# Linear attention with a gated unit: a list schedule that knows one engine per PSUM bank and two DMA queues, K maxima and exponentials split by bank, gate taps built on GpSimd

## The chip, the cores and the metric

The kernel runs on one core of one Trainium2 chip. The metric is the device time of one execution in microseconds (us). Lower is better. Before the change the median of three runs was 279.94 us (273.2 to 291.83).

The engines are named as the profile names them. PE is the matrix engine, and PEld is its weight load. DVE is the vector engine, ACT the scalar engine, and POOL is GpSimd. SP only issues transfers here. PSUM is the memory that PE writes into. The kernel divides it into eight banks, and a piece of work takes one or two of them.

A run is called slow when it is more than 1.5% above the fastest of its kernel.

## The reference

Eight batches, eight heads, 576 rows, head size 64. Both q and k are mapped to 256 positive features, and linear attention follows. Its result goes through a gated unit with a causal convolution of five taps.

```python
def phi(x):
    proj = np.einsum('bhsd,df->bhsf', x, w_phi)
    proj = proj - np.max(np.abs(proj), axis=-1, keepdims=True)
    return np.concatenate([np.exp(proj), np.exp(-proj)], axis=-1)
q_p, k_p = (phi(q), phi(k))
kv  = np.einsum('bhsf,bhsd->bhfd', k_p, v);  z = np.sum(k_p, axis=2)
num = np.einsum('bhsf,bhfd->bhsd', q_p, kv)
den = np.einsum('bhsf,bhf->bhs', q_p, z)[..., None] + 1e-06
x = num / den                  # transposed to (batch, row, 512)
for k in range(5):
    gate_pre += conv_w[k][None, None, :] * xp[:, k:k + S, :]
out = (1 / (1 + np.exp(-gate_pre)) * (x @ w_val)) @ w_out
```

## The kernel before

The kernel is a program with a planner in it. Each piece of work is entered with its engine, an assumed cost, a priority and the buffers that it touches. A list scheduler then simulates the engines and fixes the order of every engine's instructions. Nothing of that is left at run time: each engine runs its own fixed list, in order.

A priority is made of the batch number times a period, plus a number per stage (`TURN`). The planner before assumed one transfer at a time, and it did not know that the program keeps two engines from being in one PSUM bank together:

```python
TURN = dict(
    kload=-55.6, qload=-18.1, vload=-18.1, wload=6.4, k=-4.5, q=1.3, kexp=-1.7, vs=-21.0, mqt=1.7, qp=10.0,
    kv=17.7, num=5.3, xt=16.6, gate=21.4, val=27.7, out=25.8,
)
# ... in Plan.run():
                    if o.dma:
                        dma_free = max(dma_free, now + cost + self.DMA_LAT - 1.0) + o.dma
                        end = dma_free + 1.0
```

The features of k come in five groups per batch, four whole ones and a tail of half the size. PE writes a group into two banks. DVE takes its absolute maximum, and ACT takes exp(+) and exp(-) of it. Each of the three instructions reads both banks:

```python
        def k_max(u, ps):
            # ...
            nc.vector.tensor_reduce(
                mem(MK[grp[u]])[:, 1, o:o + 2 * nx].rearrange("p (x t) -> p t x", t=2),
                mem(ps)[:, :, 0:nx * F].rearrange("p t (x f) -> p t x f", f=F),
                AX.X, ALU.max, apply_absolute_value=True)
        def k_exp(u, ps, sgn):
            # ...
            nc.scalar.activation(
                mem(KE[u])[:, sgn, :, :].rearrange("p (x t) f -> p t x f", t=2),
                mem(ps)[:, :, 0:nx * F].rearrange("p t (x f) -> p t x f", f=F), AF.Exp, scale=1.0 - 2.0 * sgn)
```

POOL scales v with exp of the negated maxima (`VT`), PE multiplies (`kv`), and so on to the output product. POOL also issues the loads that cast to bf16. For batches after the first, a load writes rows of k or q to a scratch (`KR`, `QR`), and SP issues a transposing transfer from there (`KT<-KR`). The first batch is transposed on PE, and DVE copies the result (`KT<-PS`). The taps of the gate (`GW`) are four multiplies made once, on DVE.

## Time and profile before

The profiled run took 274.97 us (a fast one), with a span of 273.1. These are lines of its page: busy time and share per engine; busy tenths in 40 equal slices; the granted clock in tenths; the busy share of the DMA engines; and the engines of the chain that ended last.

```profile
span 273.1 us, 8666 instructions
...
PE 216.7 (79%) x3756; PEld 165.4 (61%) x3756; DVE 176.5 (65%) x273; ACT 178.1 (65%) x234; POOL 113.6 (42%) x184
...
PE   0256758599988997979878997979798989898881
...
PEclk9999999979979998999989997999999999999998
DMA  7999999923999389818999779937960130022005
...
PE 40%; DVE 34%; ACT 10%; issue 7%; POOL 3%; DMA 1%; ACTq 1%; DVEq 0%
```

No engine is full, and the chain wanders between PE, DVE and ACT. The waits between them decide. The output product of the eight batches starts at 65.5, 94.8, 124.5, 154.5, 184.1, 212.7, 239.8 and 263.0 us. So the span is 65.5 us of start, seven steps (29.3, 29.7, 30.0, 29.6, 28.6, 27.1, 23.2), and 10.1 us at the end.

Here is a part of one batch, from the timeline of DVE before. The columns are start, length, engine, line, operation, output and inputs; the brackets give the idle time just before and what ended it.

```profile
175.42 1.22 DVE L476 TENSOR_REDUCE MK_83<-PS 128x8 f32<-128x1024 f32 x1
...
177.45 1.22 DVE L552 TENSOR_REDUCE MQ_100<-PS 128x8 bf16<-128x1024 f32 x1
180.22 0.69 DVE L476 TENSOR_REDUCE MK_83<-PS 128x4 f32<-128x512 f32 x1 [1.55 <-ACT KEt_80 L484]
```

And the timeline of ACT before in the same stretch:

```profile
176.73 1.94 ACT L484 ACTIVATE KE_74<-PS 128x1024 bf16<-128x1024 f32 x2 [1.25 <-DVE MK_83 L476]
178.55 0.66 ACT L747 ACTIVATE GS_127<-PS 128x576 bf16<-128x576 f32 x1
179.08 1.11 ACT L484 ACTIVATE KEt_80<-PS 128x512 bf16<-128x512 f32 x2
```

DVE and ACT take turns on the same group. ACT stands 1.25 us until the maximum of 175.42 has ended, and DVE stands 1.55 us until the exponentials of the tail have ended. The waits of PE between 70 and 245 us hold the same thing as a sum (total us, times, longest):

```profile
PE PS L446 <- ACT KE_74 L484: 6.1, 5, 1.4
PE PS L684 <- issue: 3.3, 3, 1.5
```

PE cannot write the next group until ACT has left the banks. "issue" is a stall that no instruction explains.

The start, on DVE: the taps come first, and the first maximum of k is at 17.37 us.

```profile
8.32 3.57 DVE L324 TENSOR_TENSOR GW<-ID_190,CO 128x768 bf16<-128x768 f32 x4
11.80 1.28 DVE L393 COPY KT_65<-PS 128x1024 bf16<-128x1024 bf16 x1
...
17.37 2.35 DVE L476 TENSOR_REDUCE MK_81<-PS 128x8 f32<-128x1024 f32 x2 [1.73 <-ACT KE_73 L484]
```

### The profile page before, as it was taken

The numbers are of one execution on the slowest core, as the hardware profiler recorded it, in microseconds if no ns is written. First come the engines' busy times: TensorE is split into PE (matmuls) and PEld (weight loads), VectorE is DVE, ScalarE is ACT, GpSimd is POOL, SyncE is SP. The second block draws the span as 40 slices with busy tenths as digits, with TensorE's granted clock in tenths as the row PEclk, the third lists the DMA queues.
The fourth block names the chain that finished last, engine by engine and source line by source line (L and its number), as shares of the span: only waits on it lengthen the run. The fifth ranks groups of instructions, "written<-read, shape, count | busy, mean of one in ns | idle before, by whom it ended". The sixth has DMA issues, their size and how long they took to land.

```text
span 273.1 us, 8666 instructions
## 1 busy us (share of the span) xinstructions
PE 216.7 (79%) x3756; PEld 165.4 (61%) x3756; DVE 176.5 (65%) x273; ACT 178.1 (65%) x234; POOL 113.6 (42%) x184
## 2 busy tenths in 40 slices
PE   0256758599988997979878997979798989898881
PEld 0244457466676766765756677666676577657750
DVE  2869407786479918875677837972897479726340
ACT  2048750498777797569947795689757995785311
POOL 8952790069134462419034735145142606260000
PEclk9999999979979998999989997999999999999998
DMA  7999999923999389818999779937960130022005
GB/s 95 139 274 246 167 157 265 157 51 93 226 206 191 72 208 270 195 25 192 204 200 179 160 188 246 120 89 186 239 100 0 72 105 2 4 87 92 2 0 173
DMA packets 59456, 38.80 MB, mean 142 GB/s; under 512 B 37402, under 2 KB 51098, under 8 KB 59354
## 3 DMA queue, kind: packets, MB, share of 16 engines
q1 hardware_dynamic: 47328, 25.37, 40.9%
q0 software_dynamic: 12000, 12.86, 28.6%
q8 instruction: 29, 0.48, 0.7%
q14 instruction: 9, 0.07, 0.1%
q10 hardware_dynamic: 90, 0.02, 0.0%
HBM read 30.49 MB, written 17.69 MB: 176 GB/s over the span
## 4 chain that ended last, share of the span: by engine, by line
PE 40%; DVE 34%; ACT 10%; issue 7%; POOL 3%; DMA 1%; ACTq 1%; DVEq 0%
PE PS L783 11%; PE PS L640 6%; PE PS L741 5%; PE PS L684 4%; DVE MK_82 L476 4%; PE PS L446 3%; PE PS L752 3%; ACT KE_74 L484 3%; DVE MK_81 L476 3%; DVE XN_117 L695 2%; DVE MQ_98 L552 2%; DVE MK_83 L476 2%; DVE MQ_100 L552 2%; DVE MQ_99 L552 2%; DVE XP_122 L724 2%
## 5 line engine op out<-in xcount | busy, mean ns | idle before, releaser
L484 ACT ACTIVATE KE_73<-PS 128x1024 bf16<-128x1024 f32 x16 | 15.7, 1028 | 30.4 <-PE PS L446 22.5
L752 PEld LDWEIGHTS <-WVAL 64*128 64x128 bf16 x512 | 26.9, 94 | 4.0 <-issue 0.6
L741 PEld LDWEIGHTS <-GW 128*64 128x64 bf16 x384 | 23.0, 115 | 7.2 <-issue 4.7
L476 DVE TENSOR_REDUCE MK_81<-PS 128x8 f32<-128x1024 f32 (+1 forms) x15 | 16.6, 1110 | 5.3 <-ACT KE_73 L484 2.0
L484 ACT ACTIVATE KE_74<-PS 128x1024 bf16<-128x1024 f32 x16 | 15.5, 1024 | 5.9 <-DVE MK_82 L476 2.6
L660 DVE CAST KVS_112<-PS 128x520 bf16<-128x520 f32 x8 | 5.2, 695 | 20.7 <-PE PS L652 17.3
L476 DVE TENSOR_REDUCE MK_82<-PS 128x8 f32<-128x1024 f32 (+1 forms) x13 | 14.2, 1096 | 6.0 <-PE PS L446 2.4
L752 PE MATMUL PS<-XP_122,WVAL 64*128 64x288 bf16 x256 | 17.9, 282 | 0.2 <-DVE MQ_100 L552 0.2
L503 POOL TENSOR_SCALAR MK_83<-MK_83 128x16 f32<-128x16 f32 (+1 forms) x5 | 1.3, 252 | 40.3 <-DVE MK_83 L476 28.7
L752 PE MATMUL PS<-XP_123,WVAL 64*128 64x288 bf16 x256 | 17.7, 282 | 0.0
L747 ACT ACTIVATE GS_124<-PS 128x576 bf16<-128x576 f32 x8 | 5.2, 655 | 18.9 <-PE PS L741 17.9
L741 PE MATMUL PS<-XP_123,GW 128*64 128x288 bf16 x192 | 15.2, 308 | 1.7 <-DVE XP_123 L724 1.0
L741 PE MATMUL PS<-XP_122,GW 128*64 128x288 bf16 x192 | 15.0, 297 | 1.5 <-DVE XP_122 L724 1.0
L476 DVE TENSOR_REDUCE MK_83<-PS 128x8 f32<-128x1024 f32 (+1 forms) x12 | 13.5, 1130 | 3.2 <-ACT KEt_80 L484 1.6
L503 POOL TENSOR_SCALAR MK_82<-MK_82 128x20 f32<-128x20 f32 (+1 forms) x5 | 1.3, 252 | 32.6 <-DVE MK_82 L476 32.6
L589 PEld LDWEIGHTS <-EB 64*128 64x128 bf16 x256 | 11.2, 100 | 4.2 <-issue 1.0
L609 ACT ACTIVATE QE_104<-PS 128x1024 bf16<-128x1024 f32 x12 | 11.8, 1032 | 1.7 <-PE PS L589 1.7
L552 DVE TENSOR_REDUCE MQ_100<-PS 128x8 bf16<-128x1024 f32 (+1 forms) x12 | 12.5, 1042 | 0.6 <-ACT GS_127 L747 0.3
L552 DVE TENSOR_REDUCE MQ_99<-PS 128x8 bf16<-128x1024 f32 (+1 forms) x12 | 12.4, 1041 | 0.5 <-PE PS L446 0.5
L609 ACT ACTIVATE QE_105<-PS 128x1024 bf16<-128x1024 f32 x12 | 11.7, 1030 | 1.5 <-PE PS L589 1.5
L446 PE MATMUL PS<-W_173,QT_67 64*128 64x128 bf16 x144 | 9.1, 242 | 4.4 <-issue 1.6
L660 DVE CAST KVS_113<-PS 128x520 bf16<-128x520 f32 x8 | 5.3, 695 | 10.6 <-PE PS L652 10.6
(284 smaller groups left out, 712.5 us busy)
## 6 DMA issues: line engine op xcount, KB each, us to landing
KR_141<-in_k_dram POOLq DMA_DIRECT2D x7, 512.0 KB, 8.0
QR_143<-in_q_dram POOLq DMA_DIRECT2D x7, 512.0 KB, 9.8
VN_69<-in_v_dram SPq DMA_DIRECT2D x6, 512.0 KB
VN_70<-in_v_dram SPq DMA_DIRECT2D x6, 512.0 KB, 4.1
out_dram<-OS_136 SPq DMA_DIRECT2D x9, 256.0 KB, 7.9
out_dram<-OS_138 SPq DMA_DIRECT2D x8, 256.0 KB, 4.2
out_dram<-OS_137 SPq DMA_DIRECT2D x7, 256.0 KB, 7.1
VN_69<-in_v_dram POOLq DMA_DIRECT2D x2, 512.0 KB, 8.3
```

What stands on the lines that cost most here:

```text
L446: nc.tensor.matmul(ps[:, par, F * x:F * x + F], Tt[ROWS[par], cols], W2[ROWS[par], :], start=True, stop=True,)
L476: nc.vector.tensor_reduce(mem(MK[grp[u]])[:, 1, o:o + 2 * nx].rearrange("p (x t) -> p t x", t=2), mem(ps)[:, :, 0:nx * F].rearrange("p t ( ...
L484: nc.scalar.activation(mem(KE[u])[:, sgn, :, :].rearrange("p (x t) f -> p t x f", t=2), mem(ps)[:, :, 0:nx * F].rearrange("p t (x f) -> p ...
L552: nc.vector.tensor_reduce(mem(MQ[j])[:, :].rearrange("p (t s) -> p t s", t=2)[:, :, o:o + n], mem(ps)[:, :, 0:n * F].rearrange("p t (x f) ...
L589: nc.tensor.matmul(mem(ps)[:, par, P * x:P * x + P], EB[ROWS[par], 4 * g + x, :], mem(MQS[j])[ROWS[par], :], start=False, stop=(x == 3), s ...
L609: nc.scalar.activation(mem(QE[u])[:, sgn, :, :, :], mem(ps).rearrange("p t (x i) -> p t x i", x=4), AF.Exp, scale=1.0 - 2.0 * sgn,)
L640: nc.tensor.matmul(mem(ps)[:, xi, c0:c0 + E1], mem(KE[u])[:, sgn, s, :], mem(VT[u])[:, sgn, s, :], start=(g == 0 and sgn == 0 and jp == 0) ...
L660: nc.vector.tensor_copy(mem(KVS)[:, 2 * xp:2 * xp + 2, :, :, :].rearrange("p x g s e -> p x (g s e)"), mem(ps)[:, :, 0:4 * E1],)
L684: nc.tensor.matmul(mem(ps)[0:m, g, x * E1:(x + 1) * E1], lhsT, mem(KVS)[:, x, g, sgn, :], start=(sgn == 0), stop=(sgn == 1),)
L741: nc.tensor.matmul(mem(ps)[ROWS[x], po, 0:HALF], GW[:, 2 * jt + x, po, s, :], mem(XP)[:, 2 * jt + x, s:s + HALF], start=(s == 0), stop=(s ...
L752: nc.tensor.matmul(mem(ps)[:, par, 0:HALF], WVAL[ROWS[par], h, jt * P:(jt + 1) * P], mem(XP)[ROWS[par], h, PAD:PAD + HALF], start=(h == 0) ...
L783: nc.tensor.matmul(mem(ps)[:, n, :], rows(jt)[:, P * c:P * c + P], WOUT[:, jt, :], start=(jt == 0), stop=(jt == 3),)
```

## The change

The intent is a better order, made possible by better knowledge in the planner. In its model a piece of work may not start while another engine is in its bank, and two DMA queues share the DMA engines, each of two transfers at half speed. K maxima and exponentials are halved, one bank each, so that DVE and ACT work on one group at the same time. The taps move from DVE to POOL. The copies of the first batch's K become contiguous, and the K groups read other columns to match. The priorities and some assumed costs were tuned anew. The core of the diff, with cuts:

```diff
+    def _transfers(self, until):
+        while True:
+            heads = [q for q in self.queues.values() if q and q[0][1] <= self.dma_now + 1e-9]
+            # ... each head moves at 1/len(heads) of full speed
+    def _can(self, o):
+        for t, k in o.banks:
+            for e, end in t.touch[k].items():
+                if e != o.eng and end > self.now:
+                    return False
+        return all(self._place(t) is not None for t in o.takes)
@@ priorities
-    kload=-55.6, qload=-18.1, vload=-18.1, wload=6.4, k=-4.5, q=1.3, kexp=-1.7, vs=-21.0, mqt=1.7, qp=10.0,
-    kv=17.7, num=5.3, xt=16.6, gate=21.4, val=27.7, out=25.8,
+    taps=2.5, kload=-50.4, qload=-16.3, vload=-11.0, wload=6.4, k=-4.5, q=1.3, kexp=-2.9, vs=-21.0, mqt=4.6,
+    qp=10.0, kv=17.3, num=5.3, xt=17.3, gate=21.4, val=27.5, out=35.3,
@@ taps
-            plan.op("DVE", 0.9, _At((0, "k", 10.0)), lambda jt=jt: build_gw(jt), w=[gw], after=[o])
+            plan.op("POOL", 1.55, _At((0, "taps", 3.0)), lambda jt=jt: build_gw(jt), w=[gw], after=[o])
@@ copies of the first K
-                mem(tok)[:, 8 * P * hh:8 * P * hh + 8 * P].rearrange("q (x i j) -> q x j i", x=4, j=2),
+                o.rearrange("q (x i j) -> q x j i", x=4, j=2) if i else o.rearrange("q (x j i) -> q x j i", x=4, j=2),
@@ K groups
-            plan.op("DVE", 1.13 * c, at("kexp") + p0, lambda u=u, ps=ps: k_max(u, ps), r=[ps], w=[MK[grp[u]]],
-                    takes=[MK[grp[u]]] if u in (0, 2) else [])
-            for sgn in range(2):
-                plan.op("ACT", 0.94 * c, at("kexp") + p0, lambda u=u, ps=ps, s=sgn: k_exp(u, ps, s), r=[ps], w=[KE[u]])
+            for par in range(2):
+                plan.op("DVE", 0.6 if u < 4 else 0.34, at("kexp") + p0, lambda u=u, ps=ps, p=par: k_max(u, ps, p),
+                        r=[ps], w=[MK[grp[u]]], takes=[MK[grp[u]]] if u in (0, 2) and par == 0 else [], bank=par)
+            for par in (1, 0):
+                for sgn in range(2):
+                    plan.op("ACT", 0.477 if u < 4 else 0.26, at("kexp") + p0,
+                            lambda u=u, ps=ps, s=sgn, p=par: k_exp(u, ps, s, p), r=[ps], w=[KE[u]], bank=par)
```

## The prediction

> **What bounds it now.** No engine is full: the page's first part has PE busy 79%, DVE 65%, ACT 65% of 273.1 us. The chain that ended last runs through PE 40%, DVE 34%, ACT 10%, issue 7%: waits between in-order queues. Key-value products start every 29.3, 29.6, 28.6 and 27.1 us (stretches 130 to 244.6 us); a stretch holds about 25 us of PE records, 20.6 of DVE, 22 of ACT.
>
> In the chain of one batch (159 to 189 us) PE is absent from 167.8 to 184.1 us: XN, XP, MQ_98, MK_83, MQ_98, MK_83 on DVE, two KE_74 exponentials (1.94 us) on ACT, the tail's exponentials (1.0), its maximum (0.69), then GV and the output product. DVE and ACT take turns on a K group: a maximum of 1.22 us and two exponentials of 1.94, 3.2 us in series, because they share PSUM banks. The Trainium skill ("PSUM — Partial Sum Buffer", PSUM bank collisions) says that two engines on one bank and quadrant collide even when both read; the trace agrees in that the waits view has MK waiting for KE and KE for MK, over 15 us in all. The old schedule planned them side by side.
>
> **What the change does.**
> 1. K group by bank: ACT takes bank 1 while DVE takes bank 0, then they swap; 3.2 us in series becomes about 2.1. Cost: a pair of 128x512 exponentials takes 1.11 us against 1.94, so halves add about 0.15 us a group, 0.6 to 0.7 us of ACT per batch; a 128x512 maximum is 0.69 against 1.22, so 0.4 to 0.7 us of DVE per batch. It should remove most of the 3.6 us in which DVE stands behind KE_74 and KEt. I count 2.3 us per batch, 16 us over seven.
> 2. Start: four GW multiplies (3.57 us on DVE, 8.3 to 11.9) hold up the first KT copy, whose transposes were done near 8.6. They go to POOL, an estimated 1.55 us each from its 1.04 for 128x512. The KT copies become contiguous (1.28 us to about 0.68, as the XP copy of that size). POOL scales the first two V groups before the second maximum, not after; VT now runs 29.0 to 38.6. I count 5 us.
> 3. The rest: PE's steady sequence is nearly the old one. I count 0. Matmuls and bytes are unchanged. The drain (28.5 us) gains nothing.
>
> **Sum.** 273 - 16 - 5 = 252 us for a fast run. Two of three runs before were 2.5% and 7% above their fastest, so I add some: **256 us**, 8 in 10 within **246 to 268**. Faster by over 2%: 0.91; within 2%: 0.07; slower: 0.02.
>
> **What would show it.** Step 1: the period falls from 29 to about 26.5 us; K maxima and exponentials overlap in the timeline; DVE's wait for KEt goes and PE's wait for KE_74 (6.1 us) shrinks; ACT busy rises 5 to 6 us. Step 2: first K maximum at about 13 us, not 17.4; first key-value product complete near 35 us, not 41. Step 3: PE busy about the same.
>
> **What would make it wrong.** DVE, in order, waits on the bank that ACT holds, so each group costs 2.1 us of DVE time; ACT at 23 us a batch becomes the limit; late K loads or a lower PE clock (0.93 in the middle) set the period; or POOL's GW and DMA issues delay the first V scaling. Each would leave 260 to 268 us.

## The result, and the profile after

The median is 254.25 us (252.89 to 254.88, four runs) against 277.89 of before (273.2 to 291.83, four runs). The ratio is 0.9255, with a 95% interval of 0.9152 to 0.9358: faster. Ratios in this text are the mean time of one kernel's fast runs over that of the other's fast runs of the same rounds, so they are not quite the ratios of the medians.

The same lines of the page after (profiled run 253.82 us, fast):

```profile
span 252.0 us, 8796 instructions
...
PE 208.8 (83%) x3756; PEld 159.4 (63%) x3756; DVE 172.4 (68%) x311; ACT 183.0 (73%) x314; POOL 118.9 (47%) x186
...
PE   0766577989879998999899989998899989897980
...
PEclk9999997999999999999999999999999999999997
DMA  7989999947997089995959999979910500040005
...
DVE 44%; PE 41%; ACT 6%; issue 5%; POOL 1%; ACTq 0%; DVEq 0%; POOLq 0%
```

ACT is 4.9 us busier, the price of the halves. PE is 7.9 us less busy with the same 3756 records, most of which the clock explains: summed over stretches of 1 us, what the granted clock took away is worth 9.6 us of full clock before and 3.1 after (1.1 and 1.4 of these lie at the very end, when PE's work is done). The output products now start at 59.2, 85.3, 112.5, 139.2, 165.5, 192.3, 218.6 and 241.9 us. The steps are 26.1, 27.2, 26.7, 26.3, 26.8, 26.3 and 23.3 us. So of the 21.1 us between the two spans, 6.3 come before the first output product, 14.8 in the seven steps, and none at the end (10.1 us in both).

The same part of a batch in the timeline of DVE after:

```profile
158.15 0.68 DVE L524 TENSOR_REDUCE MK_83<-PS 128x4 f32<-128x512 f32 x1
159.02 0.75 DVE L810 SCALAR_TENSOR_TENSOR GV_128<-GS_124,PS 128x576 bf16<-128x576 bf16 x1 [0.19 <-PE PS L803]
159.69 0.22 DVE L626 COPY MQS_102<-PS 128x128 bf16<-128x128 bf16 x1
159.83 0.68 DVE L524 TENSOR_REDUCE MK_83<-PS 128x4 f32<-128x512 f32 x1
```

And in that of ACT after:

```profile
158.23 2.06 ACT L532 ACTIVATE KE_74<-PS 128x512 bf16<-128x512 f32 x4
```

The two maxima of the group stand at 158.15 and 159.83, around ACT's four exponentials of 158.23 to 160.29. While ACT is in the bank that the second maximum needs, DVE does other work, a gate product and a copy. In this stretch DVE runs from 146.53 to past 167 us with gaps of 0.19 and 0.24. Of the waits of PE between 63 and 224 us none sums to more than 1.2 us; the 6.1 us behind KE_74 are gone. What is left is one idle time of DVE per batch, while PE makes the output product and the next key-value product. In the waits after:

```profile
DVE KVS_113 L711 <- ACT OSt_139 L873: 10.3, 2, 5.1
DVE KVS_112 L711 <- ACT OSt_140 L873: 10.3, 2, 5.1
```

The steps themselves, with one stretch of each kernel from one key-value product to the next (two of before, then one of after; the columns are length, busy us of PE, PEld, DVE, ACT and POOL with their instructions, granted clock, DMA share, GB/s):

```profile
159.20:188.80 29.60, 25.87 (x469) 19.75 (x465) 20.63 (x31) 22.11 (x30) 11.99 (x20) 0.94 0.81 161
188.80:217.40 28.60, 24.72 (x467) 18.58 (x465) 20.44 (x31) 22.09 (x30) 10.36 (x16) 1.00 0.46 99
```

```profile
143.90:170.20 26.30, 24.31 (x467) 18.38 (x466) 20.50 (x36) 22.62 (x40) 12.55 (x21) 1.00 0.99 198
```

The work of an engine hardly differs; the step is shorter by 2.3 to 3.3 us. But both stretches of before also hold an issue stall of PE (1.49 and 1.13 us), and the first a stretch at half clock (0.94 against 1.00). What is left without these stands in the table at the end of the experiments. After, PE's records fill 24.3 of 26.3 us, so I expect little more here from order alone; no run tests that.

The start, in the timeline of DVE after:

```profile
8.66 0.69 DVE L440 COPY KT_65<-PS 128x1024 bf16<-128x1024 bf16 x1 [0.27 <-PE PS L433]
10.46 0.69 DVE L440 COPY KT_65<-PS 128x1024 bf16<-128x1024 bf16 x1 [1.10 <-PE PS L433]
...
11.94 2.48 DVE L524 TENSOR_REDUCE MK_81<-PS 128x4 f32<-128x512 f32 x4 [0.59 <-PE PS L494]
```

The timeline of POOL after, which now makes the taps and then issues the next load of q:

```profile
13.42 2.91 POOL L366 TENSOR_TENSOR GW<-ID_190,CO 128x768 bf16<-128x768 f32 x2
...
16.54 2.89 POOL L366 TENSOR_TENSOR GW<-ID_190,CO 128x768 bf16<-128x768 f32 x2
19.38 0.67 POOL L407 DMA_DIRECT2D QR_143<-in_q_dram  x1
```

The first maximum of k is 5.4 us earlier, at 11.94. Yet the first key-value product starts at the same time, 33.5 us against 33.4, because something new stands ahead of it. These lines are for the transposed K of the second batch, before and then after (count, ns minimum/median/maximum, first and last start in us):

```profile
L446 PE MATMUL PS<-W_173,KT_66 x36: 212/216/311, 50.5 to 59.5; 64*128 64x128 bf16 x36
L374 SPq DMA_TRANSPOSE KT_66<-KR_141 x1: 9155/9155/9155, 16.2 to 16.2; - x1
```

```profile
L494 PE MATMUL PS<-W_173,KT_66 x36: 213/274/311, 28.6 to 38.7; 64*128 64x128 bf16 x36
L420 SPq DMA_TRANSPOSE KT_66<-KR_141 x1: 3174/3174/3174, 17.5 to 17.5; - x1
```

The K groups of the second batch begin at 28.6 us instead of 50.5. They used to interrupt the first batch's gate, and now 20 of the 36 matmuls are done before the first key-value product. The transfer that they need held SP for 3.17 us instead of 9.15. This goes with the new order, and it hangs on a transfer. The first key-value product then runs without a gap, 33.5 to 37.1 us, where before it waited twice for POOL's scaled v and took until 40.9. POOL's scaling of v begins at 23.6 us instead of 29.0.

### The profile page after: what moved, and what is told of

It reads as the page before. It is cut to its first block, busy times and chain, and to the rows that moved or that the text cites. A ratio compares the mean times of both kernels' runs of the same rounds, so it can differ in the third digit from the quotient of the medians.

```text
span 252.0 us, 8796 instructions
## 1 busy us (share of the span) xinstructions
PE 208.8 (83%) x3756; PEld 159.4 (63%) x3756; DVE 172.4 (68%) x311; ACT 183.0 (73%) x314; POOL 118.9 (47%) x186
## 4 chain that ended last, share of the span: by engine, by line
DVE 44%; PE 41%; ACT 6%; issue 5%; POOL 1%; ACTq 0%; DVEq 0%; POOLq 0%
PE PS L834 11%; PE PS L691 6%; PE PS L792 6%; PE PS L803 6%; DVE MQ_100 L603 3%; DVE MK_82 L524 3%; DVE MQ_99 L603 3%; DVE XN_117 L746 3%; DVE MK_81 L524 2%; DVE XP_123 L775 2%; DVE XP_122 L775 2%; DVE MQ_97 L603 2%; PE PS L494 2%; DVE MK_83 L524 2%; DVE XN_119 L746 2%
## 5 line engine op out<-in xcount | busy, mean ns | idle before, releaser
L803 PEld LDWEIGHTS <-WVAL 64*128 64x128 bf16 x512 | 25.5, 94 | 8.2 <-issue 4.1
L532 ACT ACTIVATE KE_73<-PS 128x512 bf16<-128x512 f32 x32 | 16.7, 615 | 17.7 <-PE PS L494 15.3
L792 PEld LDWEIGHTS <-GW 128*64 128x64 bf16 x384 | 21.7, 109 | 4.8 <-issue 3.1
L524 DVE TENSOR_REDUCE MK_81<-PS 128x4 f32<-128x512 f32 (+1 forms) x30 | 17.8, 627 | 3.5 <-PE PS L494 3.1
L532 ACT ACTIVATE KE_74<-PS 128x512 bf16<-128x512 f32 x32 | 16.9, 612 | 0.0
L524 DVE TENSOR_REDUCE MK_83<-PS 128x4 f32<-128x512 f32 (+1 forms) x24 | 14.5, 634 | 2.8 <-PE PS L494 2.8
L524 DVE TENSOR_REDUCE MK_82<-PS 128x4 f32<-128x512 f32 (+1 forms) x26 | 15.6, 620 | 1.0 <-PE PS L494 0.8
L792 PE MATMUL PS<-XP_123,GW 128*64 128x288 bf16 x192 | 13.8, 287 | 1.3 <-DVE XP_123 L775 1.0
L660 ACT ACTIVATE QE_104<-PS 128x1024 bf16<-128x1024 f32 x12 | 11.7, 1038 | 4.4 <-PE PS L640 4.4
L792 PE MATMUL PS<-XP_122,GW 128*64 128x288 bf16 x192 | 13.9, 288 | 0.4
L660 ACT ACTIVATE QE_105<-PS 128x1024 bf16<-128x1024 f32 x12 | 11.8, 1028 | 1.9 <-PE PS L640 1.7
L660 ACT ACTIVATE QE_106<-PS 128x1024 bf16<-128x1024 f32 x10 | 10.0, 1060 | 1.4 <-PE PS L640 1.4
## 6 DMA issues: line engine op xcount, KB each, us to landing
VN_69<-in_v_dram SPq DMA_DIRECT2D x6, 512.0 KB, 10.4
```

The lines of the kernel that those rows point to most:

```text
L524: nc.vector.tensor_reduce(mem(MK[grp[u]])[:, 1, o + par:o + 2 * nx:2].unsqueeze(2), mem(ps)[:, par, 0:nx * F].rearrange("p (x f) -> p x f" ...
L532: nc.scalar.activation(mem(KE[u])[:, sgn, par:2 * nx:2, :], mem(ps)[:, par, 0:nx * F].rearrange("p (x f) -> p x f", f=F), AF.Exp, scale=1. ...
L660: nc.scalar.activation(mem(QE[u])[:, sgn, :, :, :], mem(ps).rearrange("p t (x i) -> p t x i", x=4), AF.Exp, scale=1.0 - 2.0 * sgn,)
L792: nc.tensor.matmul(mem(ps)[ROWS[x], po, 0:HALF], GW[:, 2 * jt + x, po, s, :], mem(XP)[:, 2 * jt + x, s:s + HALF], start=(s == 0), stop=(s ...
L803: nc.tensor.matmul(mem(ps)[:, par, 0:HALF], WVAL[ROWS[par], h, jt * P:(jt + 1) * P], mem(XP)[ROWS[par], h, PAD:PAD + HALF], start=(h == 0) ...
```

## The experiments

Twelve kernels ran, in four sets, each beside the kernel before on the same chip; all gave correct results. "After" in the edits is the changed kernel. Medians are of four runs. The steps between output products come from each profiled run. Sets ran on different chips, so I compare medians of different sets only for differences of several us, and read the steps and the start from the traces. Ratios are to the fast runs of the kernel before.

**e1_whole.** After's order, with each K group's work issued whole: the maximum in the place of its first half, the exponentials in the place of their last half.

```diff
         def k_max(u, ps, par):
+            if par == 1:
+                return
-                mem(MK[grp[u]])[:, 1, o + par:o + 2 * nx:2].unsqueeze(2),
+                mem(MK[grp[u]])[:, 1, o:o + 2 * nx].rearrange("p (x t) -> p t x", t=2),   # k_exp likewise
```

> The changed kernel in its own order, but each K maximum and each K exponential is issued undivided over both banks, at the place of the first half maximum and of the last half exponentials. Theory (the halves side by side bring the steady part): the period goes back to 28.5 to 29.5 us and the time to 266 to 272 us; DVE waits for KEt and KE again. Rival (the new order brings it, the halves nothing): 253 to 258 us.

Measured: 266.62 us (266.11 to 267.1), span 264.7. The first output product starts at 62.8, and the steps are 27.6, 27.9, 27.8, 27.8, 28.1, 27.8 and 24.9. The time is the one expected; the steps grew less than expected (28.5 to 29.5). Under the new order the halves are therefore worth 12.7 us of span (264.7 less 252.0): 3.6 at the start and 9.1 in the steps, 0.7 to 1.7 us in each, and 1.5 between steps free of stalls (27.8 against 26.3). In the trace PE, POOL and SP keep after's order exactly. The order was tuned for halves, and that may be part of this loss.

**e2_norule.** After's planner without the rule of one engine per bank. The bank waits of the program itself stay; only the plan ignores them.

```diff
-                if e != o.eng and end > self.now:
+                if False and e != o.eng and end > self.now:
```

> The changed kernel, planned without the rule that two engines may not be on one bank; halves, priorities and transfer model as changed. Its order differs from the changed kernel's in few places. Theory (the halves matter, not the rule): 252 to 257 us. Rival (the planner's knowledge of banks brings the gain): 260 us or more.

Measured: 260.39 us (258.95 to 262.44), span 257.8, first output at 59.4, steps 26.6, 27.8, 27.1, 27.1, 29.8, 26.6 and 23.2. The number is the rival's. By the medians the rule is worth about 6 us. Without it the plan puts two maxima of a group in a row, and DVE stands for the bank that ACT still holds, for example:

```profile
131.06 1.29 DVE L524 TENSOR_REDUCE MK<-PS 128x4 f32<-128x512 f32 x2 [0.22 <-ACT KE L532]
...
134.31 0.69 DVE L524 TENSOR_REDUCE MK<-PS 128x4 f32<-128x512 f32 x1 [0.24 <-ACT KE L532]
```

That makes some 0.5 us a batch. The step of 29.8 is a different thing: it holds an issue stall of PE of 1.87 us that ends at 181.8 us and a stretch at half clock after it, of the kind that ends this section. It alone is 3.0 of the 5.8 us between the spans of e2 and after, so of the 6 us only about half is seen to come from the order itself.

**e5_halves_old.** Before, with its planner and priorities, and only the K groups halved.

```diff
-            plan.op("DVE", 1.13 * c, ..., lambda u=u, ps=ps: k_max(u, ps), ...)      # two exps likewise
+            for par in range(2):
+                plan.op("DVE", 0.6 if u < 4 else 0.34, ..., lambda u=u, ps=ps, p=par: k_max(u, ps, p), ...)
```

> The kernel before with its old planner and priorities, and only the K maxima and exponentials split by bank. Theory: most of the steady gain without anything else, 260 to 266 us, a period near 27 us. Rival (order): 272 us or more, since the old planner places the halves blindly and there are more instructions.

Measured: 268.41 us (267.51 to 269.1). The first output product starts at 65.2, as before (65.5), and the steps are 29.9, 28.7, 27.1, 27.2, 27.2, 27.1 and 24.8. It missed the expected 260 to 266. The start gains nothing and the first two steps little; the later steps come near the expected 27. How much of that is the halves' own is another matter: before's steps hold stalls and half-clock stretches that these don't (see the table below). At the same granted clock, 0.987 to 0.99, before's fastest run took 270.54 and e5 267.51 and 268.63, so the halves alone gain 2 to 3 us.

**e6_start_old.** Before, with only the changes of the start: taps on POOL, contiguous copies, the clearing of XP moved to DVE.

```diff
-            plan.op("DVE", 0.9, _At((0, "k", 10.0)), lambda jt=jt: build_gw(jt), w=[gw], after=[o])
+            plan.op("POOL", 1.55, _At((0, "k", 10.0)), lambda jt=jt: build_gw(jt), w=[gw], after=[o])
```

> The kernel before with its old planner and priorities, and only the start changed: gate taps multiplied on GpSimd, KT copied contiguously in the first batch, the two small memsets on DVE. Theory: the first output product starts 4 to 6 us earlier and the periods stay, so 268 to 271 us. Rival (the new planner orders the start, the moved work brings little): 273 us or more.

Measured: 277.4 us (276.29 to 284.53); the first output product starts at 72.2, later than before. The expectation of 268 to 271 was wrong. The first copy of K was earlier, at 9.7 us, but the key-value product still waited 2.9 and 1.5 us for POOL's scaled v. Then the old planner, given new costs, put the second batch's K groups in the middle of the attention of the first. The saved DVE time did not reach the output.

**e9_ops_old.** Both of these together: every changed instruction, under the old planner and priorities. The edit is that of e5 and e6.

> Before's planner, its one-transfer model and its old priorities, with all the changed instructions (K groups split by bank, gate taps on POOL, contiguous KT copies, memsets on DVE): all of the change except the order. Theory (the moved instructions gain fully only under the new planner and priorities): 264 to 270 us, steady steps about 27, first output product at 62 to 70. Rival (the prediction's step 3: the order counts nothing, the two instruction changes make the gain): 256 us or less.

Measured: 278.07 us median of four, two of them slow; the fast ones are 267.47 and 271.3, ratio 0.9859 (0.9649 to 1.0069). The profile fell into a slow run, so its lines are not compared. The fast runs lie where the halves alone were. The rival, that the instructions make the gain and the order counts nothing, is refuted: no run came near 256. All that this kernel lacks is the new planner and its priorities and costs, and its two fast runs are 13 to 17 us above after's median (their clocks were 0.975 and 0.971, after's 0.98 to 0.988).

**e7_turn_old.** After's planner and instructions, with the priorities of before.

```diff
-    taps=2.5, kload=-50.4, qload=-16.3, vload=-11.0, ... mqt=4.6, ... xt=17.3, ... val=27.5, out=35.3,
+    taps=0.5, kload=-55.6, qload=-18.1, vload=-18.1, ... mqt=1.7, ... xt=16.6, ... val=27.7, out=25.8,
```

> The changed kernel and its planner with the old stage priorities (taps 0.5). Theory (halves, the bank rule and the start carry the gain, not the retuned priorities): 253 to 258 us. Rival (the new priorities carry it): 262 us or more.

Measured: 270.4 us (263.32 to 273.13); its one fast run took 263.32 and three were slow, the profiled one among them. Fast against fast, the tuned priorities carry about 9 us, by one run. The better planner with the old priorities gets only part of the way.

**e8_dma_old.** After, planned with one transfer at a time instead of two queues that share.

```diff
-                        self.queues[e].append([o, now + cost + self.DMA_OUT, o.dma])
+                        self.dma_free = max(self.dma_free, now + cost + 1.0) + o.dma
+                        self._ended(o, self.dma_free + 1.0)
```

> The changed kernel, planned with the old model of one transfer at a time, so Q loads are issued among the V scalings. Theory (the moment of the loads decides whether PE's next block of instructions arrives late, and a late one costs up to 1.8 us of idle PE and then 3.4 us at half clock): more PE gaps put down to issue than the one of 0.7 us after 100 us in the changed kernel, more half-clock stretches, 257 to 263 us. Rival (the transfer model does nothing): 252.5 to 255.5 us and as many stretches.

Measured: 258.5 us (257.76 to 259.45), ratio 0.9414 (0.9331 to 0.9496). The first output product starts at 62.5, and the steps are 28.4, 27.1, 26.3, 26.3, 26.3, 25.9 and 23.4. The loss of 4 us is at the start and in the first step, where the loads are; later steps are as good as after's. The two-queue model pays only there. The time is the one expected, but not the cause: the idea that the model also avoids late blocks of instructions fell with this, since there was one issue stall, of 0.8 us.

**e10_same_bank.** After, with the exponentials starting on the same bank as the maxima.

```diff
-            for par in (1, 0):
+            for par in (0, 1):
```

> The changed kernel with the exponentials of the two banks issued in the order of the maxima (bank 0 first), so that ACT follows DVE instead of starting on the other bank; halves, rule and priorities stay and the planner plans anew. Theory (working side by side is what counts): each group starts its exponentials 0.6 us later, 256 to 261 us. Rival (it is the finer grain alone): 252.5 to 255.5 us.

Measured: 255.33 us (254.14 to 255.56), ratio 0.9288 (0.921 to 0.9365), later steps 26.3. The number is the rival's. To start on opposite banks is worth about 1 us, and the later steps gain nothing from it. The finer grain is enough: the engines follow each other one half behind.

**e3_gw_dve.** After, with the taps back on DVE.

```diff
-            plan.op("POOL", 1.55, _At((0, "taps", 3.0)), lambda jt=jt: build_gw(jt), w=[gw], after=[o])
+            plan.op("DVE", 0.9, _At((0, "taps", 3.0)), lambda jt=jt: build_gw(jt), w=[gw], after=[o])
```

> The changed kernel with only the four gate-tap multiplies put back on DVE, where the planner sets them ahead of the first KT copy again. Theory (they held up the start by 3 us): the first KT copy starts near 11.9 us instead of 8.7, the first output product 2.5 to 3.5 us later, 256.5 to 258 us, periods unchanged. Rival (GpSimd's scaling of V sets the start, not the first copy): within 1 us of 254.

Measured: 272.55 us (268.98 to 280.38; the fast ones 268.98 and 269.98). The expectation was 256.5 to 258, so this was the largest miss of all, well beyond either theory. Four multiplies of 0.9 us cost 15 us. This is from POOL's waits between 10 and 45 us in e3's profiled run, a fast one:

```profile
POOL KR L407 <- DMA KT<-KR: 8.5, 1, 8.5
```

And this from its chain in order of time (start, length, what):

```profile
15.42 20.19 DMA KT<-KR
```

Freed of the taps, POOL issued the next loads at once: `QR` at 12.72 us instead of 19.38, and both weight matrices from 15.69 instead of 20.58. They went out beside the transposing transfers of the second batch's K, a large one (`KR`) and one for the tail (`KRt`). The trace has no landing of the large one, so I compare the tail's, in the views of DMA issues from 10 to 40 us (the last column is us from issue to landing; after first, then e3):

```profile
KT_66<-KRt_142 SPq DMA_TRANSPOSE x1, 7.2
```

```profile
KT<-KRt SPq DMA_TRANSPOSE x1, 12.0
```

From the issue of the large one to the landing of the tail it is 10.4 us after and 20.4 in e3. PE's fixed list has those K groups ahead of the first key-value product. PE stood 3.6 us for them, and POOL stood 8.5 us before it could issue the next K, with two of the four whole groups of v still to scale behind that.

So I had two causes in one experiment: DVE is held up by 3.6 us, and POOL issues loads early. From about 65 us on, PE's order is another one too, because the planner had read the new cost. The next kernel takes them apart.

**e11_gw_both.** After, with the taps multiplied on DVE as in e3 and used from there, while POOL multiplies the same into a scratch that nobody reads.

```diff
+    GX = const.tile([P, H, 2, 3, D], BF16, name="GX")
-            plan.op("POOL", 1.55, _At((0, "taps", 3.0)), lambda jt=jt: build_gw(jt), w=[gw], after=[o])
+            plan.op("POOL", 1.55, _At((0, "taps", 3.0)), lambda jt=jt: build_gw(jt, nc.gpsimd, GX), after=[o])
+            plan.op("DVE", 0.9, _At((0, "taps", 3.0)), lambda jt=jt: build_gw(jt), w=[gw], after=[o])
```

> After's kernel in which DVE too multiplies the gate taps (four multiplies ahead of its first KT copy, and these are the ones used), while POOL still does the same four multiplies, at the same place in its order, into a scratch tile that nobody reads. So DVE is held up as in e3_gw_dve and POOL's loads are issued as late as after. Theory (e3 lost its 18 us because POOL, freed early, issued its loads early, and these delayed the K transpose of the second batch; DVE's hold-up is worth only some 3 us): 256 to 260 us, first KT copy near 12, first K maximum near 15, no wait of POOL for the K transpose over 3 us, steps of the output product 26 to 27. Rival (DVE's hold-up at the start is itself what costs): 266 us or more, like e3.

Measured: 257.52 us (255.78 to 259.25), ratio 0.9425 (0.9318 to 0.9531). Useless work on POOL made the kernel some 12 us faster than e3's fast runs. In the trace every engine keeps after's order, but for DVE's four added multiplies (and eight matmul records that are missing). The loads went out at 20.82 us and later, and the large transposing transfer held SP for 4.09 us:

```profile
16.34 4.09 SPq L423 DMA_TRANSPOSE KT<-KR  x1
```

The tail's landed after 6.5 us:

```profile
KT<-KRt SPq DMA_TRANSPOSE x1, 6.5
```

That is 10.7 us from the issue of the large one, against 10.4 after.

DVE's hold-up alone is worth about 3 us (257.52 against 254.25). POOL's work also keeps the next loads back, by 8 us for `QR`, while the K of the second batch is being transposed. Of the 10.7 us between the spans of e3 and e11, 4.8 are there at the first output product, and these are what the early loads are shown to cost. Most of the rest is in one step of 32.4 us, which holds an issue stall of PE of 4.6 us, of the kind described at the end of this section; whether the early loads or the other order led to it stays open.

**e4_kt_step.** After, with the copies of the first batch's K strided again, and the planner told so.

```diff
-            plan.op("DVE", 1.2 if i else 0.6, prio, lambda ps=ps, hh=hh: cp(ps, hh), r=[ps], w=[tok],
+            plan.op("DVE", 1.2, prio, lambda ps=ps, hh=hh: cp(ps, hh), r=[ps], w=[tok],
```

> After's kernel with the first batch's KT copies strided again (1.28 us each, as before, in place of 0.69) and its first K units read contiguous columns accordingly. Theory: only the start moves, by two copies of 0.6 us at most on the chain to the first K maximum: 254.5 to 256 us, first K maximum near 12.6 to 13.2, steady steps as after. Rival (small shifts of the start set off a larger loss through the loads, as in e3 and e8): 258 us or more.

Measured: 258.52 us (257.93 to 258.85), ratio 0.9459 (0.9391 to 0.9527). The number is the rival's. But the first K maximum came at 11.96 us, as after (11.94), and the first two steps grew to 28.8 and 29.0 (26.1 and 27.2 after). Told other costs, the planner had made another order, from the first K groups on. Each of the two steps also holds a stretch at half clock, of the kind described below.

**e12_kt_kept.** The same strided copies, with the planner still told 0.6 us, so that every engine keeps after's order. The traces agree: the instructions of all five engines come in the same sequence.

```diff
-                o.rearrange("q (x i j) -> q x j i", x=4, j=2) if i else o.rearrange("q (x j i) -> q x j i", x=4, j=2),
+                o.rearrange("q (x i j) -> q x j i", x=4, j=2),
```

> As e4_kt_step (first batch's KT copies strided again, about 1.25 us each in place of 0.69), but the planner is still told 0.6, so that the order on every engine is exactly after's and only the cost of two copies moves. In after's trace DVE stood idle 1.10 us between these two copies and 0.59 us before the first K maximum, so the two copies should reach it only in part. Theory (e4 lost its 4 us because its planner was given other costs and made another order; the copies themselves are worth about 1 us): first K maximum at 12.5 to 13.2, 253 to 256 us. Rival (the longer copies themselves set off the loss): 257.5 us or more, as e4.

Measured: 255.33 us (254.19 to 256.57), ratio 0.9305 (0.9223 to 0.9388). The copies took 1.29 us each, and the first K maximum came at 13.75 us, later than expected, partly because the whole start of that run was 0.6 us later. So the contiguous copies are worth about 1 us. The other 3 us of e4 came with its other plan.

**The steps as a table of two by two.** These are steps of middle batches with the same 464 matmuls, at full clock and without a stall of the kind described below. Before's own trace has no such step: its shortest with all the work took 28.6 us, with a stall of 1.1. So e6, which has its planner, priorities and whole groups, stands in.

| K groups | planner and priorities of before | of after |
|---|---|---|
| whole | 27.5 (e6, its one such step) | 27.8 (e1) |
| halved | 27.1 to 27.2 (e5) | 26.3 (after) |

Here are one step of e6, one of e5 and one of e1 (columns as in the stretches above):

```profile
186.54:214.08 27.54, 24.68 (x467) 18.73 (x465) 20.19 (x32) 22.24 (x30) 10.65 (x18) 1.00 0.39 115
```

```profile
151.03:178.18 27.15, 24.87 (x468) 18.69 (x465) 20.51 (x37) 22.68 (x40) 13.12 (x22) 1.00 0.95 196
```

```profile
145.99:173.75 27.76, 24.76 (x464) 18.81 (x464) 20.23 (x32) 22.20 (x30) 12.60 (x21) 1.00 1.00 208
```

The halves are worth 1.5 us a step under the new order, but only about 0.4 under the old one. The order is worth 0.8 with halves and nothing with whole groups. So in a step without stalls the gain of about 1.2 us belongs to the two together. Over the six full steps that makes about 7 of the 14.8 us, an estimate from this table. The other half goes with what follows.

**Half clock and issue stalls, seen but not tested.** In before's trace the granted clock is either full or half. A half-clock stretch lasts 3.4 us. There are five of them between 55 and 170 us before, and one after, at 41 us; each trace has one more at its very end. Each of the five follows a window of that length in which PE idled 1.4 to 2.1 us. It fits that after has fewer, since PE has fewer gaps.

The issue stalls of before (0.6 to 1.6 us of idle PE, five of them; the view of waits puts one down to ACT) each begin at the same place in a block of 256 of PE's records, after 193 of them, weight loads and matmuls counted together. Each ends 1.3 to 1.5 us after a packet of 16 KB of the instruction queue has landed. For example, such a packet starts at 162.82 us and takes 0.96, and PE goes on at 165.16:

```profile
165.16 0.51 PE L684 MATMUL PS<-KVS_112,QE_109 128*128 128x65 bf16 x6 [1.49 <-issue]
```

Two stalls are left after, of 0.41 and 0.71 us, at the same place of a block. Before's runs also scatter with the clock: in one set its fastest, 270.54 us, had 0.987 and its slowest, 290.21, had 0.941. I made no experiment that removes only these stalls or only the half clock. Four of before's steps took 29.3 to 30.0 us, about 2 more than the clean 27.5; each holds one half-clock stretch and one issue stall. So about half of the 14.8 us in the steps goes with stalls and half clock, an estimate; whether the halves, the order or chance keeps them away in after stays open.

## Why the prediction was right or wrong

The total was right: 256 us predicted, 254.25 measured, inside 246 to 268, and faster as expected. The sum got there partly by errors that cancelled, so the closeness of the number is in part luck.

- **What bounds it: right.** In-order queues that wait for each other on PSUM banks. The 6.1 us of PE behind KE_74 are gone, and so are DVE's waits behind KEt. The Trainium skill's "PSUM — Partial Sum Buffer", section "PSUM bank collisions raise a hardware error", requires the turns. No run here shows the error itself, because the kernels keep the turns.
- **Step 1, halves, "2.3 us per batch, 16 us over seven": the turns were the right place to look, but the gain is not the halves' own.** The new order with whole groups cost 12.7 us (e1), about 1.5 a step without stalls and 3.6 at the start. Under the old order the halves alone gained 2 to 3 us at equal clock (e5). The swap, "ACT takes bank 1 while DVE takes bank 0", hardly counts: the steps stay at 26.3 without it (e10). The cost side was right: ACT rose by 4.9 us for "5 to 6". The period fell to 26.1 to 27.2 for "about 26.5".
- **Step 2, the start, "I count 5 us": the size was near, the reasons only in part right.** The start gained 6.3 us. The first K maximum came at 11.94 for "about 13", the key-value product was complete at 37.1 for "near 35". V was scaled earlier, as said (23.6 for 29.0). But I also counted DVE's freed time. That is worth about 3 us for the taps (e11) and 1 for the copies (e12), and under the old planner it was worth nothing (e6). The feared sentence, "POOL's GW and DMA issues delay the first V scaling", saw half of it. Without the taps POOL starts to scale at 21.9 instead of 23.6 us (e3), but the taps also delay the loads, and that helps the transposing transfer by more (e3 against e11).
- **Step 3, "PE's steady sequence is nearly the old one. I count 0": this is the step that failed.** All of the changed instructions without the new order made 0.986 (e9). By the fast runs the new planner and its priorities are worth some 13 to 17 us over e9. Taken out singly, the bank rule is worth up to 6 us (e2), the priorities about 9 (e7), and the two-queue model 4 (e8). One effect of the order is plain in the traces: the second batch's K groups start at 28.6 us, not 50.5. These figures don't add up to the gain, since each part was taken out of a whole that had been tuned for it.
- **"PE busy about the same": wrong.** It fell by 7.9 us, with the same matmuls, and most of that (6.5 us by the sums above) is that fewer of them ran at half clock.
- **"The drain (28.5 us) gains nothing": right.** From the start of the last key-value product to the end it is 28.6 us before and 28.7 after.

## What to carry to other kernels

When the order of instructions is planned, the plan's knowledge and priorities are part of the change, and cannot be counted as nothing because the steady sequence looks alike: compare where the first two batches interleave. Work on an engine that also issues transfers acts as a spacer between them, so moving that work moves the transfers; test the two apart with useless work in the old place. And when an experiment changes a cost that a planner reads, change the instruction and keep the plan (e12), or the result is that of another plan (e4). Before a gain per step is shared out, compare steps without stalls and at the same clock: with 28.6 instead of 27.5 us for before's step the halves would have seemed worth 1.5 us under either order.

## What the Trainium skill lacked or had wrong

- "DMA: Bandwidth & Descriptors", section "Issuing engines are not separate DMA queues", says that transfers of all issuers run on the same 16 engines and interleave. The runs agree, and show a cost that the section does not give: with loads of POOL's queue issued early beside them, the two transposing transfers of one batch's K took 20.4 us from the first issue to the last landing (e3), and 10.7 or 10.4 where those loads went out 7 to 8 us later (e11, after).
- "Runtime: NRT & Kernel Launch", section "Instruction fetch mechanics", calls the cost of crossing a block of 256 instructions mostly hidden. The block size fits the trace. In the kernel before, five crossings seem not to have been hidden: PE stood 0.6 to 1.6 us. The causal link is argued from the coincidence only.
- "TensorE: Matmul & The Clock Gate", Part 1, gives a free-running window of 3413 ns and half clock after an idle window. The length fits the trace; but windows with only 1.4 to 2.1 us of idle PE were followed by half clock here, and one with as much (1.48 us, in e1) was not.
- No page that I found has what a planner would need to know here: which transfers in flight slow a transposing one, and by how much.
